# Attention followed by a multiplicative FFN: the order of the weight loads, of the weight fusion and of the first FFN chunks

## The chip, the cores and the metric

The kernel runs on one core of a Trainium2 chip. The metric is device time in microseconds (us) of one execution; lower is better. Times quoted from a profile count from the first instruction of the profiled execution.

## The reference

Inputs are float32. Batch B is 8, heads H 8, tokens S 576, head size D 64, beacons Nb 16. The FFN has 8 x 576 = 4608 tokens, d_model 512 and d_ff 1024.

```python
k_all = np.concatenate([beacon_k, k], axis=2)      # 16 + 576 keys
v_all = np.concatenate([beacon_v, v], axis=2)
scores = scale * np.matmul(q, k_all.transpose(0, 1, 3, 2))
scores = np.where(causal, -1000000000.0, scores)   # beacons are always seen
a = np.exp(scores - scores.max(-1, keepdims=True))
a /= a.sum(-1, keepdims=True) + 1e-09
attn_out = np.matmul(a, v_all)
x = attn_out.transpose(0, 2, 1, 3).reshape(B * S, H * D)
h = ((x @ w1) * (x @ w2)) @ w3
out = h @ w_out
```

## The kernel before, in words

**The FFN as a stream of units.** Nothing non-linear stands between w3 and w_out, so the kernel multiplies them once into `Wt` (`fuse`: for each of 8 row blocks of w3 eight TensorE transposes, L254, a copy by VectorE, L256, and eight matmuls, L264). Then each of nine chunks of 512 tokens needs `ff_ab` (64 matmuls with w1 and w2, L284, scaled by ScalarE, L295, multiplied by VectorE into `gT`, L297) and `ff_out` (32 matmuls with `Wt`, L305, an eviction, L315, and an output DMA of 128 rows on SP's queue, L316). These are generators that yield after every matmul. One matmul is here called a unit; there are 64 for the fusion and 96 for each chunk, 928 in all. `emit_ff(n)` issues the next n units wherever the attention code calls it.

**Attention in steps.** There are 64 steps, eight for each batch: for each pair of heads t, half 0 covers the first two query tiles and half 1 the other three. A step s issues `scores(s + 1)` (L351), its exponentials on ScalarE (L360), `values(s)` (L389, normalised by VectorE in L397 and L398) and the masks on VectorE (L372), with `fill[s]` units of the stream between them. TensorE works in this order of the program.

**Q and K transposed.** Scores need Q and K with the head size on the partitions. For batches 0 and 1, `load_pair` brings two heads at a time in float32 to tiles `st`, `cast_pair` casts them on VectorE (L157), and `pe_transpose_pair` transposes them on TensorE (L171) and copies Q by VectorE and K by ScalarE (L176, L177). From batch 2 on, `load_q` and `load_k` (L104, L113) load through POOL's queue with a cast to fp16, and `transpose_qk` issues DMA transposes on SP's queue (L128, L129), in five pairs, in steps 1 to 5 of the batch before. The attention output `x16` is transposed into `xT` by TensorE (`pe_transpose_x`, L187) for batches 0 and 1, and by DMA transposes on SP (L409) after that.

**Where the early work stands.** Step 7, the last of batch 0, is a stage of its own: it does the rest of the fusion, transposes batch 0's output, casts and transposes batch 1's Q and K with 28 units of chunk 0 between them, and issues the first scores of batch 1. The stage needs `st` of batch 1. w3 is held in the second half of `xT` (`w316`), which batches 4 to 7 write later. `LEFT` sets how many units are left for the tail after the last step: 242 in this kernel.

**Queues.** The order of the loads on POOL's queue is the order of the program: v of batch 0, w_out, w3, w1 with w2 by quarters, batch 1's pairs 0 and 1, v of batch 1, pairs 2 and 3, then q and k of batch 2. SP's queue has batch 0's pairs, and nothing more until the transposes of batch 2.

Of the kernel before, what the change touches and what calls it, by code (L numbers as in the profile page):

```python
# [12 lines left out]
ds, ts = bass.ds, bass.ts  # L13
# [26 lines left out]
def kernel(  # L40
# [13 lines left out]
    nc = tc.nc  # L54
    B, H, S, D = q.shape
    Nb = beacon_k.shape[2]
    P = 128
    NT = H // 2
    DM = H * D
    DF = moe_w3.shape[0]  # L60
    M = B * S
    NKT = DM // P
    NFT = DF // P
    NJT = 5
    RUN = 6
    NR = S // RUN
    NB2 = 2
# [4 lines left out]
    xT = const.tile([P, NKT, M], FP16, name="xT")  # L72
    w12 = const.tile([P, NKT, 2 * DF], FP16, name="w12")
    Wt = const.tile([P, NFT, DM], FP16, name="Wt")
    wo16 = const.tile([P, NFT, DM], FP16, name="wo16")
    q16s = [const.tile([P, NJT, DM], FP16, name=f"q16_{i}") for i in range(NB2)]
    k16s = [const.tile([P, NJT, DM], FP16, name=f"k16_{i}") for i in range(NB2)]
# [24 lines left out]
    def load_q(b, c):  # L102
        rows = min(P, S - c * P)
        nc.gpsimd.dma_start(  # L104
            q16s[b % NB2][:rows, c, :].rearrange("s (h d) -> s h d", h=H),
            q[b, :, ds(c * P, rows), :].rearrange("h s d -> s h d"),
        )
# [11 lines left out]
    def load_k(b, jt):  # L119
        load_kv(b, jt, k, beacon_k, k16s[b % NB2][:, jt, :].rearrange("s (h d) -> s h d", h=H))  # L120
# [11 lines left out]
    early_qk, early_b = {}, {}  # L132

    def load_pair(b, t):
        engine = nc.gpsimd if b else nc.sync
        for i, src in enumerate((q, k)):
            st = early.tile([P, 2, RUN * D], FP32, name="st")
            engine.dma_start(
                st[:NR], src[b, ds(2 * t, 2)].rearrange("h (p j) d -> p h (j d)", j=RUN)
            )  # L140
            early_qk[b, t, i] = st
        if t == 0:
            bst = bkp.tile([Nb, H, D], FP32, name="bst")
            engine.dma_start(bst, beacon_k[b].rearrange("h n d -> n h d"))
            early_b[b] = bst

    o16s = {}
# [15 lines left out]
    def pe_transpose_pair(b, t):  # L163
        qT, kT = qTs[b % NB2], kTs[b % NB2]
        for o16, dst, off, copy in (
            (o16s[t][0], qT, 0, nc.vector.tensor_copy),
            (o16s[t][1], kT, Nb, nc.scalar.copy),
        ):
            pt = psM.tile([P, 1024], FP16, name="pm")
            for j in range(RUN):  # L170
                nc.tensor.transpose(pt[:, ds(j * NR, NR)], o16[:NR, j, :], ident[:NR, :NR])  # L171
            if off:
                nc.tensor.transpose(
                    pt[:, ds(S, Nb)], early_b[b][:, ts(t, P)], ident[:Nb, :Nb]
                )
                copy(dst[:, t, 0:Nb], pt[:, ds(S, Nb)])  # L176
            copy(  # L177
                dst[:, t, ds(off, S)].rearrange("p (i j) -> p i j", j=RUN),
                pt[:, 0:S].rearrange("p (j i) -> p i j", j=RUN),
            )  # L180
# [27 lines left out]
    for t in range(NT):  # L208
# [6 lines left out]
        fill=0.0,  # L215
# [17 lines left out]
        )  # L233
    for c in range(NJT):
        load_v(0, c)
    wo_v = moe_w_out.rearrange("(a c p) n -> a p c n", p=P, c=2)
    for a in range(4):
        nc.gpsimd.dma_start(wo16[:, ds(2 * a, 2), :], wo_v[a])

    w316 = xT[:, :, ds(M // 2, 2 * DF)].rearrange("p a (c r) -> p a c r", c=2)  # L240
    for kt in range(NFT):
        nc.gpsimd.dma_start(w316[:, kt // 2, kt % 2], moe_w3[ts(kt, P), :])
    for c in range(4):
        for i, w in enumerate((moe_w1, moe_w2)):
            nc.gpsimd.dma_start(
# [4 lines left out]
    def fuse():  # L250
        def w3_transposed(kt):
            pt = psM.tile([P, NFT, P], FP16, name="pm")
            for rt in range(NFT):
                nc.tensor.transpose(pt[:, rt, :], w316[:, kt // 2, kt % 2, ts(rt, P)], ident)  # L254
            wT = wp.tile([P, NFT, P], FP16, name="wT")
            nc.vector.tensor_copy(wT, pt)  # L256
            return wT

        wT = w3_transposed(0)
        for kt in range(NFT):  # L260
            nxt = w3_transposed(kt + 1) if kt + 1 < NFT else None
            pm = psM.tile([P, DM], FP32, name="pm")
            for rt in range(NFT):
                nc.tensor.matmul(  # L264
                    pm,
                    wT[:, rt, :],
                    wo16[:, rt, :],
                    start=(rt == 0),
                    stop=(rt == NFT - 1),
                )  # L270
                if rt < NFT - 1:
                    yield
            nc.scalar.copy(Wt[:, kt, :], pm)  # L273
            wT = nxt
            yield

    def ff_ab(mc):
        gT = gp.tile([P, NFT, 512], FP16, name="gT")
        for kf in range(NFT):
            a_sb = None  # L280
            for i in range(2):
                pm = psM.tile([P, 512], FP32, name="pm")
                for kt in range(NKT):
                    nc.tensor.matmul(  # L284
                        pm,
                        w12[:, kt, ds(i * DF + kf * P, P)],
                        xT[:, kt, ds(mc * 512, 512)],
                        start=(kt == 0),
                        stop=(kt == NKT - 1),
                    )  # L290
                    if kt < NKT - 1:
                        yield
                if i == 0:
                    a_sb = asb.tile([P, 512], FP32, name="a_sb")
                    nc.scalar.activation(a_sb, pm, AF.Copy, scale=GS)  # L295
                else:
                    nc.vector.tensor_tensor(gT[:, kf, :], pm, a_sb, ALU.mult)  # L297
                yield
        return gT
# [17 lines left out]
            yield  # L317

    def stream():
        yield from fuse()  # L320
        for mc in range(M // 512):
            gT = yield from ff_ab(mc)
            yield from ff_out(mc, gT)

# [3 lines left out]
    def emit_ff(n):  # L328
        nonlocal emitted
        for _ in range(n):  # L330
            try:
                next(ff)
            except StopIteration:
                return
            emitted += 1
# [28 lines left out]
    def mask(s, j):  # L364
        g = 2 * (s % 2) + j
        pT = pTs[s // 2]
        if g == 1:
            return
        m = {0: MA, 2: MB, 3: MB[:, 0:80]}[g]
        n = m.shape[1]  # L370
        blk = pT[:, :, ds(GO[g], n)]
        nc.vector.tensor_tensor(  # L372
            blk, blk, m.unsqueeze(1).to_broadcast([P, 2, n]), ALU.mult
        )
# [37 lines left out]

    NSB = 2 * NT
    NS = B * NSB
    LEFT = 50
    n_first = 28
    n_kept = 10
    n_second = 96 - n_first - n_kept
    fill = [0] * NS
    fill[6] = 8  # L420
    for s in range(NSB, 2 * NSB):
        fill[s] = n_second * (s - NSB + 1) // NSB - n_second * (s - NSB) // NSB
    rest, n = n_kept + 6 * 96 - LEFT, NS - 2 * NSB
    for s in range(2 * NSB, NS):
        fill[s] = rest * (s - 2 * NSB + 1) // n - rest * (s - 2 * NSB) // n

# [11 lines left out]
    cast_pair(0, 3)  # L438
    pe_transpose_pair(0, 3)
    constants(1)  # L440
    for i in range(NB2):
        nc.vector.memset(k16s[i][64:128, 4, :], 0.0)
        nc.vector.memset(q16s[i][64:128, 4, :], 0.0)
    for t in range(2):
        load_pair(1, t)
    for c in range(NJT):
        load_v(1, c)
    for t in range(2, NT):
        load_pair(1, t)
    for c in range(NJT):  # L450
        load_q(2, c)
        load_k(2, c)
    for s in range(NS):
        b, r = s // NSB, s % NSB
        if s == NSB - 1:
            values(s)
            emit_ff(16)
            pe_transpose_x(0)
            emit_ff(64 - emitted)
            cast_pair(1, 0)  # L460
            for t in range(NT):
                emit_ff(n_first // NT)
                pe_transpose_pair(1, t)
                if t + 1 < NT:
                    cast_pair(1, t + 1)
            emit_ff(64 + n_first - emitted)
            scores(s + 1)
            for j in range(2):
                exps(s + 1, j)
                mask(s + 1, j)  # L470
            continue
        if s + 1 < NS:
            scores(s + 1)
            exps(s + 1, 0)
        values(s)
        k1 = min(8, fill[s])
        emit_ff(k1)
        if s + 1 < NS:
            exps(s + 1, 1)
            mask(s + 1, 0)  # L480
        emit_ff(fill[s] - k1)
        if s + 1 < NS:
            mask(s + 1, 1)
        if s == 2 * NSB - 1:
            pe_transpose_x(1)
        if 1 <= b < B - 1:
            if r == 0:
                for c in range(NJT):
                    load_v(b + 1, c)
                for c in range(NJT if b + 2 < B else 0):  # L490
                    load_q(b + 2, c)
                    load_k(b + 2, c)
            if 1 <= r <= NJT:
                transpose_qk(b + 1, r - 1)
# [31 lines left out]
```

## Time and profile before

| What | Value |
|---|---|
| median of 13 runs | 327.01 us (322.49 to 328.68) |
| the profiled execution | 324.24 us, span 322.2 us |
| granted TensorE clock | 0.999 |
| TensorE busy | 290.7 us (90% of the span) |
| VectorE / ScalarE busy | 168.2 us / 157.8 us |
| DMA | 42.97 MB in packets, 133 GB/s mean |
| HBM read / written | 39.32 MB / 9.44 MB |

The span is the time from the first to the last instruction in the trace; the execution's own time has what lies around it too. A page of the profile also gives each engine's busy share in 40 equal slices of the span, the chain of work that ended last, the costliest groups of instructions with what they waited for, and the DMA issues. PE is TensorE, DVE is VectorE, ACT is ScalarE, POOL is GpSimd, SP is SyncE; a name with q is an engine's sequencer, where DMAs are issued.

### The profile page before, as it was taken

Reading aid. Unit: us, or ns where it says so; the run is one execution under the profiler, and the core shown is the slowest. Engines: PE = TensorE matmul, PEld = TensorE weight load, DVE = VectorE, ACT = ScalarE, POOL = GpSimd, SP = SyncE. Lnnn points to the kernel's source line nnn. Section 1 sums busy time; section 2 is a strip of 40 time slices with the busy share of each in tenths; the row PEclk is TensorE's granted clock in tenths of the full one; section 3 lists DMA queues with packets and bytes.
Section 4 is the critical chain, followed back from the end, with each engine's and each line's share of the span. In section 5 each row is a group of like instructions: output and inputs, shape, how many; then the busy total and the mean of one; then the engine's idle time right before and its main releaser. Section 6 shows DMA issues by size and latency. Waiting matters only on the chain.

```text
span 322.2 us, 6961 instructions
## 1 busy us (share of the span) xinstructions
PE 290.7 (90%) x2800; PEld 151.6 (47%) x2800; DVE 168.2 (52%) x387; ACT 157.8 (49%) x229; POOL 114.0 (35%) x152
## 2 busy tenths in 40 slices
PE   1687899698999996999998999899999989999995
PEld 1465554344554443445554545454445544444442
DVE  4756335755655553555654665555555653343342
ACT  2484324577466653555566556564764452230320
POOL 8446469964493067306910970320000000000000
PEclk9999999999999999999999999999999999999999
DMA  8999999999999979998999999997451112302103
GB/s 189 204 208 206 196 219 201 145 134 139 146 193 150 121 83 176 173 141 104 197 167 164 113 207 178 105 158 146 91 75 67 65 36 61 111 0 86 44 2 130
DMA packets 155824, 42.97 MB, mean 133 GB/s; under 512 B 142976, under 2 KB 149632, under 8 KB 155792
## 3 DMA queue, kind: packets, MB, share of 16 engines
q0 software_dynamic: 102912, 19.67, 79.0%
q1 hardware_dynamic: 52880, 22.85, 39.2%
q8 instruction: 22, 0.36, 0.5%
q14 instruction: 10, 0.08, 0.1%
HBM read 39.32 MB, written 9.44 MB: 151 GB/s over the span
## 4 chain that ended last, share of the span: by engine, by line
PE 64%; DMA 18%; ACT 5%; DVE 5%; issue 3%; SPq 3%; POOL 2%; DVEq 0%; POOLq 0%
PE pm L284 30%; PE pm L305 18%; PE pv L389 9%; PE ps L351 6%; ACT pT L360 3%; DMA va<-in_v_dram 3%; DMA st<-in_q_dram 3%; DMA w<-in_moe_w_dram 3%; DMA xT<-in_moe_w_dram 3%; DMA out_dram<-ot 2%; DMA qT<-q 2%; DVE gT L297 2%; ACT a_sb L295 2%; DMA st<-in_k_dram 1%; SPq L129 1%
## 5 line engine op out<-in xcount | busy, mean ns | idle before, releaser
L284 PE MATMUL pm<-xT,w 128*128 128x512 f16 x576 | 132.8, 379 | 1.1 <-DMA xT<-x 1.0
L360 ACT ACTIVATE pT<-ps 128x736 f16<-128x736 f32 (+3 forms) x128 | 105.9, 863 | 35.8 <-PE ps L351 35.1
L295 ACT ACTIVATE a_sb<-pm 128x512 f32<-128x512 f32 x72 | 43.0, 597 | 86.0 <-PE pm L284 84.2
L284 PEld LDWEIGHTS <-w 128*128 128x128 f16 x576 | 53.4, 98 | 60.1 <-issue 2.1
L297 DVE TENSOR_TENSOR gT<-pm,a_sb 128x512 f16<-128x512 f32 x72 | 49.6, 690 | 43.8 <-PE pm L284 42.7
L305 PE MATMUL pm<-Wt,gT 128*128 128x512 f16 x288 | 66.4, 379 | 0.0
L113 POOL DMA_DIRECT2D va<-in_v_dram x40 | 34.7, 879 | 70.5 <-PE pv L389 66.0
L351 PE MATMUL ps<-qT,kT 64*128 64x80 f16 (+3 forms) x704 | 40.3, 237 | 9.9 <-ACT pT L360 7.8
L389 PE MATMUL pv<-va,pT 128*128 128x65 f16 x960 | 42.6, 197 | 5.5 <-DVE pT L372 4.9
L389 PEld LDWEIGHTS <-pT 128*128 128x128 f16 x960 | 34.4, 99 | 15.9 <-DVE pT L372 9.9
L305 PEld LDWEIGHTS <-gT 128*128 128x128 f16 x288 | 27.0, 98 | 29.8 <-DVE gT L297 0.2
L397 DVE RECIPROCAL rd<-pv 128x4 f32<-128x4 f32 x64 | 12.1, 189 | 53.5 <-PE pv L389 53.4
L351 PEld LDWEIGHTS <-kT 64*128 64x128 f16 x704 | 21.8, 97 | 38.1 <-issue 34.8
L315 DVE TENSOR_SCALAR ot<-pm 128x512 f32<-128x512 f32 x36 | 24.8, 689 | 24.3 <-PE pm L305 20.0
L398 DVE TENSOR_TENSOR x<-pv,rd 128x256 f16<-128x256 f32 x64 | 31.4, 491 | 2.4
L104 POOL DMA_DIRECT2D q<-in_q_dram x30 | 26.3, 876 | 5.4 <-DMA va<-in_v_dram 2.4
L113 POOL DMA_DIRECT2D k<-in_k_dram x30 | 25.7, 858 | 4.0 <-DMA q<-in_q_dram 2.8
L372 DVE TENSOR_TENSOR pT<-pT,MB 128x512 f16<-128x512 f16 x64 | 19.2, 324 | 5.8 <-ACT pT L360 5.8
L171 PE MATMUL pm<-ident,o 96*128 96x96 f16 x96 | 7.6, 242 | 10.1 <-DVE o L157 8.6
L264 PE MATMUL pm<-wo,wT 128*128 128x512 f16 x64 | 15.0, 379 | 0.4 <-DVE wT L256 0.4
L372 DVE TENSOR_TENSOR pT<-pT,MA 128x480 f16<-128x480 f16 x32 | 12.7, 398 | 1.4 <-ACT pT L360 1.4
L273 ACT CAST Wt<-pm 128x512 f16<-128x512 f32 x8 | 4.7, 586 | 16.2 <-PE pm L264 16.2
(41 smaller groups left out, 95.2 us busy)
## 6 DMA issues: line engine op xcount, KB each, us to landing
out_dram<-ot SPq DMA_DIRECT2D x36, 256.0 KB, 2.6
va<-in_v_dram POOLq DMA_DIRECT2D x24, 128.0 KB, 6.6
q<-in_q_dram POOLq DMA_DIRECT2D x24, 128.0 KB, 8.3
k<-in_k_dram POOLq DMA_DIRECT2D x18, 128.0 KB, 9.0
xT<-in_moe_w_dram POOLq DMA_DIRECT2D x8, 256.0 KB, 10.4
w<-in_moe_w_dram POOLq DMA_DIRECT2D x8, 256.0 KB, 10.2
st<-in_q_dram SPq DMA_DIRECT2D x4, 288.0 KB, 5.5
st<-in_k_dram SPq DMA_DIRECT2D x4, 288.0 KB, 6.2
```

Of the source, the lines that this page charges most:

```text
L104: nc.gpsimd.dma_start(q16s[b % NB2][:rows, c, :].rearrange("s (h d) -> s h d", h=H), q[b, :, ds(c * P, rows), :].rearrange("h s d -> s h d"),)
L113: nc.gpsimd.dma_start(dst[ds(p0, rows)], src[b, :, ds(s0, rows), :].rearrange("h s d -> s h d"))
L284: nc.tensor.matmul(pm, w12[:, kt, ds(i * DF + kf * P, P)], xT[:, kt, ds(mc * 512, 512)], start=(kt == 0), stop=(kt == NKT - 1),)
L295: nc.scalar.activation(a_sb, pm, AF.Copy, scale=GS)
L297: nc.vector.tensor_tensor(gT[:, kf, :], pm, a_sb, ALU.mult)
L305: nc.tensor.matmul(pm, gT[:, kf, ts(mt, P)], Wt[:, kf, :], start=(kf == 0), stop=(kf == NFT - 1),)
L315: nc.vector.tensor_scalar(ot, pm, float(1.0 / GS), None, ALU.mult)
L351: nc.tensor.matmul(ps[:, hh, ds(col, n)], kT[ds(hh * 64, 64), t, ts(jt, P)], qT[ds(hh * 64, 64), t, ds(q0, n)],)
L360: nc.scalar.activation(pT[:, :, ds(GO[g], GW[g])], pss[s][j][:, :, 0 : GW[g]], AF.Exp, scale=scale)
L372: nc.vector.tensor_tensor(blk, blk, m.unsqueeze(1).to_broadcast([P, 2, n]), ALU.mult)
L389: nc.tensor.matmul(pv[:, 2 * n + hh, 0:65], pT[:, hh, ds(col, P)], va[:, jt, 2 * t + hh, 0:65], start=(jn == 0), stop=(jn == len(BLK[i]) - 1),
L398: nc.vector.tensor_tensor(x16[:, ds(tiles[0], ni), ds(t * P, P)].rearrange("p i (h d) -> p i h d", h=2), pv[:, 0 : 2 * ni, 0:64].rearrange ...
```

## The change

- On POOL's queue w1 and w2 now follow v of batch 0, then v of batch 1, then w_out and w3, then q and k of batch 2.
- Batch 1's Q, K and beacon K are loaded on SP's queue instead of POOL's, all in step 3, each `st` tile after a one-element memset by VectorE. The memsets of k16s and q16s and the loads of batch 2's q and k stand in step 3 too.
- In the prologue the Q copies of pairs 1 to 3 of batch 0 go to ScalarE.
- The stream begins with `ff_ab` of chunks 0 and 1; then come the fusion and `ff_out` of chunks 0 and 1, and after that chunk by chunk as before. In `fuse` the next row block's transposes are issued after the fourth matmul of a block instead of ahead of the first.
- Step 7 emits 30 units (84 before, and 8 in step 6), batch 1's steps 34 (58 before), batches 2 to 7 594 (536 before), and 270 are left for the tail (242 before).

```diff
     def load_pair(b, t):
-        engine = nc.gpsimd if b else nc.sync
         for i, src in enumerate((q, k)):
             st = early.tile([P, 2, RUN * D], FP32, name="st")
-            engine.dma_start(
+            if b:
+                nc.vector.memset(st[0:1, 0, 0:1], 0.0)
+            nc.sync.dma_start(
...
-            (o16s[t][0], qT, 0, nc.vector.tensor_copy),
+            (o16s[t][0], qT, 0, nc.vector.tensor_copy if b or t == 0 else nc.scalar.copy),
...
     for c in range(NJT):
         load_v(0, c)
-    wo_v = moe_w_out.rearrange("(a c p) n -> a p c n", p=P, c=2)
-    for a in range(4):
-        nc.gpsimd.dma_start(wo16[:, ds(2 * a, 2), :], wo_v[a])
-
-    w316 = xT[:, :, ds(M // 2, 2 * DF)].rearrange("p a (c r) -> p a c r", c=2)
-    for kt in range(NFT):
-        nc.gpsimd.dma_start(w316[:, kt // 2, kt % 2], moe_w3[ts(kt, P), :])
...
         for kt in range(NFT):
-            nxt = w3_transposed(kt + 1) if kt + 1 < NFT else None
...
+                if rt == 3 and kt + 1 < NFT:
+                    nxt = w3_transposed(kt + 1)
...
     def stream():
+        gTs = []
+        for mc in range(2):
+            gTs.append((yield from ff_ab(mc)))
         yield from fuse()
-        for mc in range(M // 512):
+        for mc in range(2):
+            yield from ff_out(mc, gTs[mc])
+        for mc in range(2, M // 512):
             gT = yield from ff_ab(mc)
             yield from ff_out(mc, gT)
...
-    LEFT = 50
-    n_first = 28
-    n_kept = 10
-    n_second = 96 - n_first - n_kept
+    LEFT = 270
+    n_first = 30
+    n_second = 64 - n_first
     fill = [0] * NS
-    fill[6] = 8
     for s in range(NSB, 2 * NSB):
         fill[s] = n_second * (s - NSB + 1) // NSB - n_second * (s - NSB) // NSB
-    rest, n = n_kept + 6 * 96 - LEFT, NS - 2 * NSB
+    rest, n = 64 + 96 * (M // 512) - 64 - LEFT, NS - 2 * NSB
...
     constants(1)
-    for i in range(NB2):
-        nc.vector.memset(k16s[i][64:128, 4, :], 0.0)
-        nc.vector.memset(q16s[i][64:128, 4, :], 0.0)
-    for t in range(2):
-        load_pair(1, t)
     for c in range(NJT):
         load_v(1, c)
-    for t in range(2, NT):
-        load_pair(1, t)
-    for c in range(NJT):
-        load_q(2, c)
-        load_k(2, c)
+    wo_v = moe_w_out.rearrange("(a c p) n -> a p c n", p=P, c=2)
+    for a in range(4):
+        nc.gpsimd.dma_start(wo16[:, ds(2 * a, 2), :], wo_v[a])
+
+    w316 = xT[:, :, ds(M // 2, 2 * DF)].rearrange("p a (c r) -> p a c r", c=2)
+    for kt in range(NFT):
+        nc.gpsimd.dma_start(w316[:, kt // 2, kt % 2], moe_w3[ts(kt, P), :])
     for s in range(NS):
         b, r = s // NSB, s % NSB
         if s == NSB - 1:
             values(s)
-            emit_ff(16)
             pe_transpose_x(0)
-            emit_ff(64 - emitted)
             cast_pair(1, 0)
...
-            emit_ff(64 + n_first - emitted)
+            emit_ff(n_first - emitted)
...
+        if s == 3:
+            for t in range(NT):
+                load_pair(1, t)
+            for i in range(NB2):
+                nc.vector.memset(k16s[i][64:128, 4, :], 0.0)
+                nc.vector.memset(q16s[i][64:128, 4, :], 0.0)
+            for c in range(NJT):
+                load_q(2, c)
+                load_k(2, c)
```

More of the change, by code (lines that the diff above doesn't have):

```diff
@@ L143, in load_pair @@
             bst = bkp.tile([Nb, H, D], FP32, name="bst")
-            engine.dma_start(bst, beacon_k[b].rearrange("h n d -> n h d"))
+            nc.sync.dma_start(bst, beacon_k[b].rearrange("h n d -> n h d"))
             early_b[b] = bst
```

## The prediction

> **What bounds the kernel now.** I read the page's slices first, for which resource is full in which stretch.
>
> ```profile
> PE   1687899698999996999998999899999989999995
> ...
> DMA  8999999999999979998999999997451112302103
> GB/s 189 204 208 206 196 219 201 145 134 139 146 193 150 121 83 176 173 141 104 197 167 164 113 207 178 105 158 146 91 75 67 65 36 61 111 0 86 44 2 130
> ```
>
> A slice is 8.05 us. From about slice 11 (89 us) on PE stands at 9 nearly everywhere: the second part is bound by TensorE. Ahead of it PE is at 6 to 9, and the DMA row is at 9 from the second slice on, at some 200 GB/s for 56 us and at 135 to 145 after that. So the first 80 us have two loads side by side, and the question is which of them ends last. SP's timeline, PE's timeline and the DMA issues of one stretch answer it:
>
> ```profile
> 58.05 1.28 SPq L128 DMA_TRANSPOSE qT<-q  x1
> ...
> 72.48 1.29 SPq L129 DMA_TRANSPOSE kT<-k  x1
> ```
> ```profile
> 84.27 0.55 PE L351 MATMUL ps<-qT,kT 64*128 64x128 f16 x8
> ...
> 87.22 0.59 PE L187 MATMUL pm<-ident,x 112*128 112x112 f16 x8
> ...
> 89.19 0.52 PE L351 MATMUL ps<-qT,kT 64*128 64x128 f16 x14
> ```
> ```profile
> q<-in_q_dram POOLq DMA_DIRECT2D x1, 128.0 KB, 6.4
> ```
> ```profile
> qT<-q SPq DMA_TRANSPOSE x1, 6.7
> kT<-k SPq DMA_TRANSPOSE x1, 8.3
> ```
>
> The columns are start, duration, engine. The third fence is from the issues between 51.4 and 52 us: POOL issues the first q load of batch 2 at 51.50, and 6.4 us later, at 57.9, it has landed; the first DMA transpose of batch 2 goes at 58.05, released by it. The last fence is from the issues between 72 and 73.5 us: the last K transpose, issued at 72.48, lands 8.3 us later, at 80.8. The two score groups of the first half steps of batch 2 run on PE at 84.27 and 89.19. The second holds the last key block, so it needs that last transpose. Today the transposes are done 8.4 us before PE gets there. That slack is the first number of the forecast.
>
> The tail, from the chain of waits, gives the price of a unit (one matmul of the FFN stream):
>
> ```profile
> 297.74 13.81 PE pm L284 x64
> 311.55 6.92 PE pm L305 x32
> ```
>
> 13.81/64 is 0.216 us a unit, back to back.
>
> **The change, part by part.**
>
> (1) *Units moved.* Up to the scores at 89.19 the old kernel has emitted 28 + 64 + 58 = 150 units, the new one 30 + 34 = 64. So 86 units, 86 x 0.216 = 18.6 us of PE, move behind that point. With them go the 64 transposes of w3 (L254): PE's timeline has eight of them from 34.26 to 34.71, 0.055 each, 3.5 us. Together 22.1 us that must now run after batch 2's first scores, in a part that PE bounds. LEFT and the fills only share them out: 58 units more in the steps of batches 2 to 7, 28 more in the tail.
>
> (2) *What comes earlier in exchange.* If PE alone decided, the same 22.1 us would vanish ahead of those scores, and the sum would be zero. The loads decide how much does. Ahead of batch 2's q and k lie the same transfers in both kernels: batch 0's q, k, v, w1, w2, w3, w_out, batch 1's q, k, v. The change permutes them (w1, w2 and v of batch 1 first, w_out and w3 last on POOL's queue, batch 1's q and k on SP's), but batch 2's q and k still stand last on POOL's queue, behind all of w3. The DMA row shows no hole in these 57 us that a new order could fill. So I take the first q of batch 2 to land at 57.9 again, and SP's ten transposes to land last at 80.8 again, beside the same v of batch 2 and q, k of batch 3. PE reaches the scores of 89.19 in the new kernel as early as 65 (third rival), then waits. Gain: 89.2 - 80.8 = 8.4 us instead of 22.1.
>
> Bounds of that 80.8. Early: if nothing contends, ten issues at the shortest row seen in this stretch, 1.22 to 1.29 us, from 57.9 end at 70.6, and the shortest landing of any such transpose in the trace is 2.4: 73. Late: 3 us more for batch 1's q and k sharing with w3 instead of standing ahead of v: 84. I take 80.8, since transposes and loads of the same sizes meet in the same way.
>
> (3) *Batch 1's q and k on SP, from step 3.* Nine DMAs. They wait for VectorE's one-element memsets, eight at the 65 ns of the smallest memset (L204), 0.5 us in all, at about 25 us behind the mask of L372 at 24.74. Queued behind them on SP is nothing until the transposes at 58. By the windows, SP's queue alone moves 292 GB/s (2 to 4 us), both queues together 227 (6 to 12), POOL's alone 208 (16 to 24), so the 2.4 MB are no gift but take their share. Landing between 35 and 57 us, they let step 7 end between 45 and 62; up to 60 nothing changes in the sum, as the wait of (2) covers it.
>
> On this point the Trainium skill, "DMA: Bandwidth & Descriptors", section "Issuing engines are not separate DMA queues", speaks against the change: DMAs from several engines run on the same 16 DMA engines and interleave, and a second issuer saves sequencer time alone. The 227 beside 292 and 208 agrees. By the rule the sum stays as below; were the queues additive, some 8 us would come off it.
>
> (4) *Copies and memsets moved.* Three q copies of 0.75 us (L177) go from VectorE to ScalarE in the prologue, where ScalarE's kT copy waits 12.4 us in all for PE; its own end is set by the last load of batch 0 (landed at 14). The L442 and L443 memsets (4 x 0.27) leave the front of batch 0's attention, worth at most 1.1 us there. Both lie ahead of the wait of (2), which covers them: 0. Without that cover they would be worth 1 us of gain. POOL's q and k loads of batch 2 now wait for these memsets, but POOL gets to them well after 25 us.
>
> (5) *Fusion inside batch 2.* Its w3 copies (L256, 0.69 each) now queue on VectorE among masks. PE is given four units, 0.86 us, to cover one. Cost per copy between 0 and 0.5, the nearest row being PE's 0.4 us wait for the first of them; I take 0.2 x 8 = 1.6 (0 to 4).
>
> (6) *Stalls that may go.* PE's waits after 89 us:
>
> ```profile
> PE pv L389 <- DVE pT L372: 2.2, 1, 2.2
> PE ps L351 <- DMA qT<-q: 1.1, 1, 1.1
> PE pm L284 <- DMA xT<-x: 1.0, 1, 1.0
> ```
>
> The first is an output that SP sent late behind five transposes of x; the others are transposes that PE overtook. With 12.4 instead of 11.2 units a step, and each chunk's products further behind its batch's x, all three may go: -4.3 (bounds -4.3 and 0).
>
> *Sum*, on the profiled execution (span 322.2, its time 324.2): scores at 80.8, plus the 233.0 that follow 89.2 today, plus 22.1, minus 4.3, plus 1.6, is 333.2. That is 11.0 over. The execution lies 2.8 below the median of the runs, so the median goes from 327.0 to **338**.
>
> **Rivals.** *Forecast: batch 2's q and k set the pace*, 338, slower. For it: full DMA slices, the slack of only 8.4 us. Against: nothing but the spread of when those loads land.
>
> *Rival 1: the transposes run nearly unhindered*, scores at 73 or a little below. 73 + 233.0 + 22.1 - 4.3 + 1.6 = 325.4, median 330; with two more us gained on the loads 328, no change. For it: the latency of a transpose is 2.4 us when the queue is free. Against: v of batch 2 and q, k of batch 3 still follow at once on POOL.
>
> *Rival 2, the other side: the DMA does not gate, the work before batch 2 does.* Batch 1's q and k land by 41, step 7 ends at 45, eight steps at 2.3 us (attention 1.3 of PE and 4.3 units) and 1.9 for x's transposes: 65.3. Then 65.3 + 252.4 = 317.7, median 322.5, faster by 1.4%. It decides from scores at 66.5 downward; break-even is at 69.8. For it: PE's idle time ahead of 89. Against: it needs the transposes to land 15 us sooner with the same bytes ahead of them.
>
> *Rival 3: step 7 becomes the wait.* Batch 1's q and k starve behind w3, land at 57 as today, step 7 ends at 62, and 62 + 20.3 = 82.3 takes the place of 80.8; with no stall recovered 339, median 344.
>
> **How the numbers follow.** Forecast 0.62, rival 3 0.15, rival 1 0.15, rival 2 0.08. The runs of this kernel spread by 1 to 2%, so about 1% is what a measurement can tell from no change. Rival 1 lies at +0.9% or below, so 0.13 of it is within 1% and 0.02 above. Slower by over 1%: 0.62 + 0.15 + 0.02 = 0.79; within 1%: 0.13; faster: 0.08. The range goes from rival 1's 330 to 345, rival 3 with a little to spare; below it lie rival 2 and the even part of rival 1.
>
> **What would show it.** Right: PE idle for over 8 us ahead of the L351 of batch 2, put down to DMA qT or kT; first L128 near 58 us; those scores near 80; DMA still at 9 in the first ten slices; the tail some 28 units, 6 us, longer. Wrong: if the first L128 of batch 2 goes at 50 or earlier, (2) has failed, and the loads were not conserved by the permutation. If PE's idle time before it is put to L157 or st, rival 3 holds.

## The result, and the profile after

| | Before | Changed |
|---|---|---|
| median | 326.26 us (48 runs) | 330.68 us (11 runs) |
| ratio to before | | 1.0158, 95% interval 1.0130 to 1.0187 |
| profiled execution | 324.24 us, span 322.2 us | 329.37 us, span 327.7 us |

The changed kernel is slower by 1.6%, or 5.5 us between the two profiled spans. The forecast was slower by 11. The page of the changed kernel, its slices (here 8.2 us each):

```profile
PE   1786878829998999999999999999999999999995
...
PEclk9997898976999999999999999999999999999999
DMA  8999999999999599989999998982630330301103
GB/s 189 206 196 203 262 223 179 125 153 155 156 137 96 66 128 181 182 159 144 170 180 138 175 150 141 174 121 66 165 29 2 110 93 0 128 2 64 64 2 128
```

The DMA row stands at 9 from the second to the thirteenth slice, nearly as before (to the fourteenth). PE has a hole, the 2 in the ninth slice (66 to 74 us), which the old kernel did not have. PEclk has low digits in the ninth and tenth slices, and also in the fourth, fifth and seventh; the old kernel had none. PE's timeline shows the hole:

```profile
65.70 1.03 PE L279 MATMUL pm<-xT,w 128*128 128x512 f16 x4
68.54 0.33 PE L351 MATMUL ps<-qT,kT 64*128 64x128 f16 x4 [1.81 <-DMA kT<-k]
73.35 0.61 PE L351 MATMUL ps<-qT,kT 64*128 64x256 f16 x4 [4.48 <-DMA qT<-q]
...
77.32 2.29 PE L188 MATMUL pm<-ident,x 112*128 112x112 f16 x20
79.54 0.52 PE L351 MATMUL ps<-qT,kT 64*128 64x128 f16 x14
```

The brackets are idle time of PE and what ended it. PE is done with batch 1's steps at 66.7 and stands still for 6.3 us, for the DMA transposes of batch 2's K and Q. The second score group of batch 2 goes at 79.54 (89.19 before). SP's timeline tells when those transposes were issued, and the DMA issues between 69.5 and 70.5 us how long the last of them took:

```profile
55.85 1.27 SPq L128 DMA_TRANSPOSE qT<-q  x1
...
69.95 1.23 SPq L129 DMA_TRANSPOSE kT<-k  x1
```
```profile
kT<-k SPq DMA_TRANSPOSE x1, 7.3
```

First issue at 55.85 (58.05 before), last landing at 69.95 + 7.3 = 77.3 (80.8 before). From the group at 79.54 to the end of the span it is 248.2 us, where the old kernel took 233.0 from 89.19. So 9.65 us are won ahead of that point and 15.2 are lost behind it.

### The profile page after: what moved, and what is told of

Its sections match the earlier page's. It is cut to its first block, busy times and chain, and to the rows that moved or that the text cites. A ratio compares the mean times of both kernels' runs of the same rounds, so it can differ in the third digit from the quotient of the medians.

```text
span 327.7 us, 6963 instructions
## 1 busy us (share of the span) xinstructions
PE 296.0 (90%) x2800; PEld 155.0 (47%) x2800; DVE 165.6 (51%) x392; ACT 160.1 (49%) x232; POOL 107.2 (33%) x143
## 4 chain that ended last, share of the span: by engine, by line
PE 76%; DMA 11%; ACT 5%; SPq 3%; DVE 2%; issue 1%; DVEq 0%
PE pm L279 33%; PE pm L300 19%; PE pv L389 10%; PE ps L351 8%; DMA st<-in_k_dram 6%; PE pm L257 4%; ACT pT L360 3%; DMA qT<-q 2%; DMA st<-in_q_dram 2%; ACT a_sb L290 1%; SPq L129 1%; SPq L128 1%; PE pm L248 1%; SPq L139 1%; DVE gT L292 1%
## 5 line engine op out<-in xcount | busy, mean ns | idle before, releaser
L279 PE MATMUL pm<-xT,w 128*128 128x512 f16 x576 | 134.3, 383 | 0.7 <-ACT xT L193 0.5
L389 PE MATMUL pv<-va,pT 128*128 128x65 f16 x960 | 44.6, 201 | 3.3 <-DVE x L398 1.5
L389 PEld LDWEIGHTS <-pT 128*128 128x128 f16 x960 | 35.9, 102 | 13.9 <-DVE pT L372 4.1
L104 POOL DMA_DIRECT2D q<-in_q_dram x30 | 25.6, 854 | 9.7 <-DMA va<-in_v_dram 3.8
L257 PE MATMUL pm<-wo,wT 128*128 128x512 f16 x64 | 16.4, 380 | 1.0 <-DVE wT L250 1.0
L172 PEld LDWEIGHTS <-o 96*128 96x128 f16 x96 | 6.2, 116 | 11.6 <-DVE o L158 9.4
```

The source lines that it names most:

```text
L104: nc.gpsimd.dma_start(q16s[b % NB2][:rows, c, :].rearrange("s (h d) -> s h d", h=H), q[b, :, ds(c * P, rows), :].rearrange("h s d -> s h d"),)
L257: nc.tensor.matmul(pm, wT[:, rt, :], wo16[:, rt, :], start=(rt == 0), stop=(rt == NFT - 1),)
L279: nc.tensor.matmul(pm, w12[:, kt, ds(i * DF + kf * P, P)], xT[:, kt, ds(mc * 512, 512)], start=(kt == 0), stop=(kt == NKT - 1),)
L389: nc.tensor.matmul(pv[:, 2 * n + hh, 0:65], pT[:, hh, ds(col, P)], va[:, jt, 2 * t + hh, 0:65], start=(jn == 0), stop=(jn == len(BLK[i]) - 1),
```

## The experiments

Theory 1 is that of the forecast: batch 2's Q and K, last in POOL's order, hold TensorE up, and what was moved behind them is added to a part that TensorE bounds. Of the 5.5 us that the forecast missed, 1.25 lie ahead of the second score group and 4.2 in the 15.2, which it had put at 19.4. "The second score group" is the one at 79.54 above. Steps are counted here by the score group that they begin with: step 51 begins with `scores(51)`. "Waits of the steps" are the length of the steps from there to the last, less units at 0.216 us, transposes at 0.055 and attention matmuls at 0.042 (scores) and 0.0345 (values), from the timeline; by this count the old kernel has 13.6 us of them and the changed one 7.7.

**Batch 2's Q and K first.**

```diff
-    for a in range(4):
-        nc.gpsimd.dma_start(wo16[:, ds(2 * a, 2), :], wo_v[a])
-    for kt in range(NFT):
-        nc.gpsimd.dma_start(w316[:, kt // 2, kt % 2], moe_w3[ts(kt, P), :])
...
                 for c in range(NJT):
                     load_v(b + 1, c)
+                if b == 1:
+                    for a in range(4):
+                        nc.gpsimd.dma_start(wo16[:, ds(2 * a, 2), :], wo_v[a])
+                    for kt in range(NFT):
+                        nc.gpsimd.dma_start(w316[:, kt // 2, kt % 2], moe_w3[ts(kt, P), :])
```

> The changed kernel, with q, k and v of batch 2 ahead of w_out and w3 on POOL's queue (these two move to the first step of batch 1, behind v of batch 2). Theory 1 (the landing of batch 2's q and k holds TensorE up ahead of batch 2, as w3 stands before them): the 4.5 and 1.8 us waits for qT and kT vanish, the clock stays full from 60 us on, the second score group of batch 2 runs at about 70.5 us instead of 79.5 (step 15 starts at 64.2, two steps of 2.5 and 3.8), span 327.7 - 9.0 = 318.7, about 1.5% faster than the kernel before. Theory 2 (the loads are hidden and the time lies in the 22 us of FFN work moved behind batch 2's start): within 1% of the changed kernel, span 326 to 329.

Median 322.80 us, ratio to before 0.9929 (0.9890 to 0.9968); 7.9 us less than the changed kernel's 330.68. PE's waits between 50 and 75 us hold no DMA any more:

```profile
PE ps L351 <- ACT pT L360: 3.5, 5, 0.9
PE pm L188 <- DVE gT L292: 0.4, 1, 0.4
PE pv L389 <- DVE pT L372: 0.2, 1, 0.2
```

The second group goes at 74.61 in its profile, and from there it is 322.9 - 74.6 = 248.3 us, as in the changed kernel (248.2). Theory 1 holds: the order of the loads set the wait, and the part behind does not depend on it. The group comes 4 us later than I expected, mostly because this execution's step 7 ended 3.3 us later (50.04, not 46.74): its first seven units took 3.15 us where the changed kernel's took 1.67, so TensorE worked at about half its pace there. The other executions of this kernel were shorter than the profiled one.

**The old load order with the new stream.**

```diff
     for c in range(NJT):
         load_v(0, c)
+    for a in range(4):
+        nc.gpsimd.dma_start(wo16[:, ds(2 * a, 2), :], wo_v[a])
+    for kt in range(NFT):
+        nc.gpsimd.dma_start(w316[:, kt // 2, kt % 2], moe_w3[ts(kt, P), :])
...
     constants(1)
+    for t in range(2):
+        load_pair(1, t)      # on nc.gpsimd again, without the memset of st
     for c in range(NJT):
         load_v(1, c)
+    for t in range(2, NT):
+        load_pair(1, t)
+    for c in range(NJT):
+        load_q(2, c)
+        load_k(2, c)
```

> The changed kernel's stream and fills with the old order and queues of all loads and the old place of the memsets (the load half of the change undone). Theory 1: batch 2's q and k stand behind the same transfers in either order, so their last transpose lands within 3 us of the changed kernel's 77.3 and of the old 80.8; but batch 1's q and k land at 57.6 instead of 44.5, step 7 ends near 60 instead of 46.7, and the second score group of batch 2 comes at 60 + 8 x 2.46 + 2.8 = 82.5 instead of 79.5: span 330 to 331, 1% slower than the changed kernel. Theory 2 (the new load order is itself worth its 13 us of earlier batch 1): span about 340.

Median 333.62, ratio 1.0234 (1.0184 to 1.0283), 2.9 us over the changed kernel. PE's waits from 28 to 85 us now name the casts of batch 1's Q and K, ahead of everything else:

```profile
PE pm L171 <- DVE o L157: 9.8, 2, 8.4
```

Step 7 ends at 61, the second group goes at 84.48, and 248.2 us follow once more. Batch 2's first transpose is issued at 57.9, 2 us from the changed kernel's 55.85. So the permutation is worth 3 us, no more: the transfers ahead of batch 2's Q and K are the same.

**The fusion back in batch 1.** It fills the hole with work that is ready.

```diff
-        for mc in range(2):
-            gTs.append((yield from ff_ab(mc)))
+        gT = yield from ff_ab(0)
         yield from fuse()
-        for mc in range(2):
-            yield from ff_out(mc, gTs[mc])
-        for mc in range(2, M // 512):
+        yield from ff_out(0, gT)
+        for mc in range(1, M // 512):
...
-    LEFT = 270
+    LEFT = 206
-    n_second = 64 - n_first
+    n_second = 128 - n_first
...
```

> The changed kernel's loads, with the fusion behind chunk 0's products in batch 1's steps (98 units there instead of 34, 594 units in batches 2 to 7 as in the changed kernel, 206 in the tail). Theory 1: the fusion fills TensorE's wait for batch 2; w3 has landed at 54.8, before it is wanted at about 57; eight steps of 3.67 and 3.5 of transposes from 46.7 bring batch 2's second score group to about 83.5 instead of 79.5, and 17.3 us less follow: span 314.4, 2.7% faster than the kernel before. Theory 2 (batch 1's steps cannot take the fusion, as VectorE's copies and ScalarE's evictions hold them up by over 10 us): span 325 or more.

Median 321.37, ratio 0.9856 (0.9802 to 0.9911). The span is 319.4, not 314.4: the second group comes at 86.17 instead of 83.5, and one stall of 3.8 us appears in step 51, where VectorE waits for an output tile. PE's line for it, from the waits between 205 and 225 us, and the chain that ended there:

```profile
PE pv L386 <- DVE pT L369: 2.1, 1, 2.1
```
```profile
208.00 0.32 DVE ot L310
208.32 6.75 DMA out_dram<-ot
...
215.16 0.69 DVE ot L310
215.85 0.33 DVE pT L369
```

Read downward: an output DMA, issued at 208.32 at the end of five transposes of x on SP, lands 6.75 us later; only then may VectorE evict the chunk's fourth output to the same tile; the mask behind it on VectorE comes 0.33 us after, and PE's values wait for that mask. It is the stall that the old kernel has in step 27. The forecast had seen it there and priced it by PE's row, 2.2 us. Here the step is 3.8 us longer than its matmuls and PE's row is 2.1 us; the rest lies behind the wait, where 13 units take 4.64 us (2.97 in step 19 of the changed kernel) at a granted clock of 0.57 (216 to 220 us):

```profile
213.63 0.52 PE L348 MATMUL ps<-qT,kT 64*128 64x128 f16 x14
216.22 0.39 PE L386 MATMUL pv<-va,pT 128*128 128x65 f16 x6 [2.08 <-DVE pT L369]
216.43 4.64 PE L279 MATMUL pm<-xT,w 128*128 128x512 f16 x13
```

**TensorE kept busy in the hole.**

```diff
+        if s == 2 * NSB - 2:
+            warm = psM.tile([P, 512], FP32, name="pm")
+            for i in range(26):
+                nc.tensor.matmul(warm, w12[:, 0, 0:P], xT[:, 0, 0:512])
```

> The changed kernel with 26 matmuls of 512 columns, written to a PSUM tile that nobody reads, at the end of step 14, in TensorE's wait for batch 2's transposes (5.6 us at full clock, from 66.7 to 72.3). Theory A (the halved clock from 69 to 79 us is caused by TensorE's idleness and stretches the work between the first and the second score group of batch 2): the granted clock stays at 1.0 from 66 to 80 us, the first group still goes at 73.3, the second at 77.3 instead of 79.5, span 325.5, 0.7% faster. Theory B (the clock is not set by idleness, or nothing waits for that work): the second group at 79.5 or later, span 327.7 or more.

Median 329.90, ratio 1.0132 (1.0090 to 1.0173), an interval that overlaps the changed kernel's; the faster time of theory A is not shown. Its first half, that the clock stays full when TensorE is busy, is. Stretches of 4 us; the column after POOL is PEclk. The changed kernel, then the one with the added matmuls:

```profile
68.00:72.00 4.00, 0.33 (x4) 0.11 (x4) 0.00 (x0) 0.79 (x1) 1.73 (x2) 0.62 1.71 150
72.00:76.00 4.00, 2.65 (x30) 1.74 (x31) 0.54 (x2) 0.14 (x1) 2.73 (x4) 0.50 1.80 155
76.00:80.00 4.00, 3.91 (x39) 2.58 (x37) 2.27 (x6) 2.45 (x5) 2.99 (x4) 0.60 2.32 156
```
```profile
68.00:72.00 4.00, 4.00 (x25) 1.86 (x22) 1.69 (x5) 0.90 (x2) 2.83 (x4) 1.00 1.82 146
72.00:76.00 4.00, 4.00 (x46) 2.01 (x44) 0.00 (x0) 0.78 (x1) 2.37 (x4) 1.00 1.73 155
76.00:80.00 4.00, 3.18 (x46) 2.02 (x43) 2.72 (x7) 3.17 (x5) 1.08 (x2) 1.00 2.03 119
```

With PE busy the granted clock stays at 1.00, and from the first group, both halves of it, to the second group it takes 78.89 - 74.57 = 4.3 us, where the changed kernel took 79.54 - 73.35 = 6.2 from the group's second half alone. But batch 2's transposes landed about 2 us later in this execution, so the second group begins only 0.65 us sooner, and its last ten matmuls wait 0.4 us for a kT again. The spans are 327.6 and 327.7 us.

**The same steps, smaller.**

```diff
-    LEFT = 270
+    LEFT = 324
```

> The changed kernel with 540 units in batches 2 to 7 instead of 594 and 324 in the tail, so 11.25 units a step, nearly the 11.2 of the kernel before. TensorE's whole work is the same; only its waits between batch 2's second score group and the last step can differ (7.7 us in the changed kernel, 13.6 in the old, counted as step length less matmuls at their back-to-back price). H1 (more units a step cover the exponentials and masks): the waits come back, spread over all batches, 12 to 14 us in all, span 332 to 334. H2 (what matters is where the four outputs of a chunk fall against the transposes of x and the v loads at a batch's end): batches without such a meeting stay at 0.5 to 1.5 us; one meeting, at steps 30 to 33, costs 3 to 4 us, span about 331.

Median 339.13, ratio 1.0357 (1.0315 to 1.0398), span 337.6: slower than either hypothesis said. The waits of the steps are 15.7 us, by batch 2.6, 1.3, 2.3, 7.6, 1.3 and 0.7; 6.0 of them lie in step 43 alone. From VectorE's waits behind 80.85 us:

```profile
DVE ot L310 <- DMA out_dram<-ot: 5.9, 2, 4.5
```

In step 43 PE itself waits 3.5 us; behind that wait the granted clock is 0.56 to 0.58 (182 to 190 us). Without that step 9.7 remain, 2 more than in the changed kernel. So the largest loss is a meeting of outputs (H2), though I had looked for it at steps 30 to 33 and it came in another batch. H1's 12 to 14 us, spread over all batches, don't come: PE's wait for exponentials in the steps is 2.2 us, as in the changed kernel (2.0).

**The old kernel with larger steps.**

```diff
-    LEFT = 50
+    LEFT = -8
```

> The kernel before with 594 units in batches 2 to 7 instead of 536 (12.4 a step as in the changed kernel) and 184 in the tail. H1 (more units a step cover the waits): the waits after batch 2's second score group fall from 13.6 us to about 8, span 322.2 - 5.9 = 316.3. H2 (the place of a chunk's outputs decides): the outputs of chunks 1 to 5 now fall at steps 22.6, 30.4, 38.1, 45.9 and 53.6, each across the end of a batch, so the 3.4 us stall of the old kernel's steps 26 and 27 returns in several batches: waits of 14 us or more, span 322 or more.

Median 333.43, ratio 1.0173 (1.0129 to 1.0217), span 333.2, and 22 us of waits of the steps. H1 had said 316.3. But the cause isn't H2's output tile either. PE's waits in the steps:

```profile
PE pm L284 <- DMA xT<-x: 12.0, 5, 3.3
PE ps L351 <- ACT pT L360: 0.7, 2, 0.5
```

The stream now asks for a chunk in the step after its batch is done, and each time TensorE waits for the DMA transposes of x. There is a second meeting point beside the outputs, and larger steps move into it. PE's wait for exponentials, 4.4 us in the old kernel, is only 0.7 here; whether the larger steps or the long waits beside them took it away can't be told from this run.

**The fusion in batch 1, and more units in step 7.**

```diff
-    LEFT = 206
-    n_first = 30
-    n_second = 128 - n_first
+    LEFT = 180
+    n_first = 56
+    n_second = 154 - n_first
```

> The kernel with the fusion in batch 1, and 56 units instead of 30 in step 7 (180 in the tail instead of 206), to fill TensorE's waits for batch 1's q and k there (7.6 us of the step's length are not matmuls). If those waits take at least half of the 5.6 us: batch 2's second score group moves from 86.2 to at most 89, with 5.6 us less to follow, so the span falls from 319.4 to 314 to 317. If the added units delay the score chain of batch 1 by their full length: 319. The stall of 3.8 us that an output causes in step 51 of that kernel may move, as each chunk's outputs come two steps sooner (H2), or stay (H1).

Median 341.13, ratio 1.0422 (1.0373 to 1.0470), a clear miss. The second group comes at 89.92, 3.75 us later for 5.6 us of units, so step 7 did hide some of them. Behind it PE waits 18.6 us for xT in five places; in the run before it was 12.0. Two steps' lead on the batches is too much.

**The old kernel with five output tiles.**

```diff
-    early = ctx.enter_context(tc.tile_pool(name="early", bufs=8))
+    early = ctx.enter_context(tc.tile_pool(name="early", bufs=7))
-    op = ctx.enter_context(tc.tile_pool(name="op", bufs=3))
+    op = ctx.enter_context(tc.tile_pool(name="op", bufs=5))
```

> The kernel before with five output tiles instead of three (and seven early tiles instead of eight, to make room). If the old kernel's stall in steps 26 and 27 (3.5 us over the matmuls) is VectorE waiting for a tile whose output DMA SP issued late behind transposes of x: DVE's 4.2 us wait for out_dram goes, PE's 2.2 us wait for the mask with it, the 1.0 us wait for xT stays, and what follows 89 us shrinks from 233.0 to about 230.5: span 319.7, 0.8% faster. If the DMA queue itself is what is late: no change.

Median 322.27, ratio 0.9839 (0.9807 to 0.9871). PE's waits from the second group to the last step (the forecast showed three lines of the old kernel's):

```profile
PE ps L351 <- ACT pT L360: 3.8, 9, 0.7
PE ps L351 <- DMA qT<-q: 0.5, 1, 0.5
PE pm L284 <- DMA xT<-x: 0.5, 1, 0.5
```

The 2.2 us wait for the mask is gone, and VectorE has no wait for out_dram left, though stores issued between 121 and 124 us still take 6.8 us to land: with more tiles, late outputs hold nobody up. The second group comes 1.9 us later (91.08); 1.5 of that is step 9, where seven units take 3.17 us instead of 1.68 (granted clock 0.65 from 64 to 68 us). Behind the group 320.1 - 91.1 = 229.0 us follow, against 233.0. Of these 4.0 us, 2.2 lie in step 27, the step of the mask, just what the row said. (The 3.5 us of the expectation are two rows: 1.0 for xT in step 26 and 2.2 for the mask in step 27.) The others lie in steps 26, 40 and 48 (0.5, 0.4 and 0.8), in waits for xT, qT and exponentials; that the tiles are their cause is not shown. The medians are 4.8 us apart (327.06 beside it), the profiled spans 2.1; why the medians differ by more, the runs don't settle.

**The changed kernel with four output tiles.**

```diff
-    qTs = [const.tile([P, NT, NJT * P], FP16, name=f"qT_{i}") for i in range(NB2)]
+    qTs = [const.tile([P, NT, S], FP16, name=f"qT_{i}") for i in range(NB2)]
-    op = ctx.enter_context(tc.tile_pool(name="op", bufs=3))
+    op = ctx.enter_context(tc.tile_pool(name="op", bufs=4))
```

> The changed kernel with four output tiles instead of three, made room for in the same way. VectorE has no wait for out_dram in the changed kernel's profile, so if late outputs are what the old kernel lost and the changed kernel no longer loses, nothing moves: span 327.7, 1.3 to 1.6% slower than the kernel before, and 2.5% slower than the kernel before with more output tiles (322.3). If it gets faster by 4 us as the old kernel did with more tiles, the output tiles do not account for the smaller difference.

Median 330.81 against the changed kernel's 330.68; span 328.6, second group at 80.45, and 248.1 us behind it. Nothing moved. The wait on an output tile that cost the old kernel 2.2 us costs the changed one nothing, with three tiles or four.

**The best version: the fusion in batch 1 and four output tiles.** On the stream and the fills of the kernel with the fusion in batch 1:

```diff
-    qTs = [const.tile([P, NT, NJT * P], FP16, name=f"qT_{i}") for i in range(NB2)]
+    qTs = [const.tile([P, NT, S], FP16, name=f"qT_{i}") for i in range(NB2)]
-    op = ctx.enter_context(tc.tile_pool(name="op", bufs=3))
+    op = ctx.enter_context(tc.tile_pool(name="op", bufs=4))
```

> The kernel with the fusion in batch 1, with four output tiles instead of three (Q's transposed buffers are cut from 640 to 576 columns to make room). If its waits for out_dram (7.3 us of VectorE in three places, PE's 3.8 us in step 51) come from the fourth output of a chunk waiting for the first one's tile, they go: span 319.4 - 3.5 = 316, against the kernel before some 3% faster. If the DMA is late as such: 319.

Median 317.64, ratio 0.9765 (0.9722 to 0.9808), span 315.8. Both theories' parts are in it: work in the hole, and outputs that hold nobody up. Its slices have the hole no more, and PEclk is full:

```profile
PE   1687898899999999999999999999999999999995
...
PEclk9999999999999999999999999999999999999999
```

Step 51 has lost its 3.8 us; the waits of the steps are 5.3 us in all.

## Why the prediction was right in its sign and wrong in its size

The sum of the forecast, against the two profiled executions:

| Term | Forecast | Measured |
|---|---|---|
| second score group earlier | -8.4 (80.8) | -9.65 (79.54) |
| units and w3 transposes moved behind it | +22.1 | the same count |
| waits recovered, less the fusion's copies | -4.3 + 1.6 = -2.7 | 15.2 - 22.1 = -6.9 |
| sum | +11.0 | +5.5 |

*(1), units moved:* right. Five kernels with this stream and these fills have 248.1 to 248.7 us behind the second group, however late it goes.

*(2), the loads:* right in mechanism and nearly in size: 9.65 us won where 8.4 were forecast. The first q of batch 2 landed 2.2 us sooner than in the old kernel, the last transpose 3.5 us sooner. The kernel with Q and K first shows that this wait was set by their place in the queue. PE was done with batch 1's steps at 66.7 us (the "65" of the forecast is worked out under rival 2, not the third), and its wait is 6.3 us, not the "over 8" that the forecast named as a sign.

*(3) and (4):* covered by the wait, as said. Step 7 ended at 46.7. The memsets moved to step 3 are not free in their place: VectorE spends 1.1 us on them between two steps and PE waits 0.8 us there for x; the hole covers it. The 8 us that additive queues would have brought didn't come: the loads ahead of batch 2 ended 2.2 us sooner.

*(5), the fusion's copies:* 1.0 us of PE's waits, near the 1.6.

*(6), the stalls that may go:* this is the step that failed, and with it the size. PE's waits from the second group to the last step, in the old kernel and in the changed one:

```profile
PE ps L351 <- ACT pT L360: 4.4, 9, 1.0
PE pv L389 <- DVE pT L372: 2.2, 1, 2.2
PE ps L351 <- DMA qT<-q: 1.1, 1, 1.1
PE pm L284 <- DMA xT<-x: 1.0, 1, 1.0
```
```profile
PE ps L351 <- ACT pT L360: 2.0, 6, 0.5
PE pm L257 <- DVE wT L250: 1.0, 1, 1.0
```

The forecast took the last three rows of the old kernel, 4.3 us, as the whole of what could be recovered. All three went, so that price was right. But it left out the first row, the largest, and so put its change at nothing without a reason: PE's wait for exponentials fell by 2.4 us. It also had nothing for the last step, which lost 1.0 us over its matmuls. 4.3 + 2.4 + 1.0, less the 1.0 of the fusion's copies, is 6.7 of the measured 6.9. Why the exponentials' wait and the last step became shorter stays open. The two runs on the size of the steps point different ways: with larger steps the old kernel's wait for exponentials fell from 4.4 to 0.7 us, but with smaller ones the changed kernel's rose only from 2.0 to 2.2; in both, other waits grew at the same time.

*The rivals:* step 7 as the wait (rival 3) and a free start of batch 2 (rival 2) didn't come. Rival 2 was possible once the order was another: the kernel with Q and K first has a median of 322.8 where I had worked out 322.5, though by a span of 317.7 where its profiled one is 322.9. The changed kernel's median, 330.7, is nearly the 330 of rival 1; that is chance, as rival 1 had the scores at 73 us, and they came at 79.54.

*A term that the sum did not have:* TensorE ran at half clock in and behind the hole. From the first group to the second the changed kernel takes about 2 us more than the one with spare matmuls; the last transpose had landed at 77.3, and the group goes at 79.54. As a shorter time this is not shown, since the spare matmuls left the span where it was.

## What to carry to other kernels

Before moving work out of a stretch, find what ends last there; if it is a transfer that the move leaves in its place, only the slack is won, and the whole of the moved work is paid where it lands. When you price the waits that a change may remove, add up all rows of the engine that bounds the time, not only those for which you have a cause: the largest was left out here. Compare the length of a step with its matmuls too: the row can be all of a stall (2.2 us in the old kernel) or half of it (2.1 of 3.8 us in step 51, with the clock at 0.57 behind the wait). And ask whether the new schedule keeps a stall: where outputs and transposes meet on one queue, about one unit more or less a step made two of these kernels 6.4 and 8.5 us slower, and 26 units more in step 7 made a third 20 us slower. When a wait can't be shortened, put ready work there: the same loads with the fusion in the hole, and one more output tile, gave 317.6 us.

## What was not expected of the hardware

The granted clock can fall to half at a wait of TensorE, and the work behind the wait is slowed. It was 0.62, 0.50 and 0.60 in the stretches from 68 to 80 us, with waits of 1.8 and 4.5 us, and 1.00 in the same stretches when 26 spare matmuls kept TensorE busy. Two more kernels with the hole, the one with four output tiles on the changed stream and the one with smaller steps, have 0.50 from 72 to 76 us too. The Trainium skill, "TensorE: Matmul & The Clock Gate", section "HAM oscillation — how this bites in real kernels", describes such a case: a wait for a DMA that crosses the activity monitor's window throttles TensorE, and the work after it starts cold, at half rate. The hole agrees with this. But long waits are not all that counts here. In the changed kernel the clock was also at 0.50 from 29 to 34 us and at 0.50 from 49 to 51 us, and no wait of TensorE in the 8 us ahead of either was longer than 0.81 us. And a wait of 2.1 us was followed by 0.57 in the kernel with the fusion in batch 1, while one of 2.2 us in the old kernel was followed by 1.00.

The old kernel's clock is 0.999 over its span, but its trace has a sign of the slower pace: behind PE's first wait, 6.4 us, twelve transposes took 1.14 us, and 0.67 at 55 us.

A store of 256 KB took 2.6 us from issue to landing at the median, but 6.8 and 7.0 us when it was issued behind five transposes of x and beside the loads of the next batch. Three tiles are enough for the first number; for the second they were too few in the old kernel and in the one with the fusion in batch 1.
